# Weights of a fused attention and Mish feed-forward kernel, loaded in quarters along the first slots

## The chip, the cores and the metric

The kernel runs on one core of one Trainium2 chip. The metric is the device time of one launch in microseconds. A core has TensorE (matmuls; in the profile PE, and PEld for its weight loads), VectorE (DVE), ScalarE (ACT), GpSimd (POOL) and SyncE (SP), each with its own queue of instructions, and 16 DMA engines that all transfers share. Here SP issues the loads of q, k and v and the stores of the output, and GpSimd issues the loads of the weights.

## The reference

```
# q, k, v: [8, 12, 448, 64] f32;  w_in: [768, 2048], w_out: [2048, 768] f32
scores = (q @ k.T) / 8
m = max(scores);  e = exp(scores - m)
attn = e / (sum(e) + exp(-m) + 1e-9)          # "softmax off by one"
o = attn @ v                                  # [8, 12, 448, 64]
x = o with heads side by side                 # [3584, 768]
h = x @ w_in                                  # [3584, 2048]
g = h * tanh(softplus(h))                     # Mish
out = g @ w_out                               # [3584, 768] f32
```

## The kernel before

A *pair* is two heads of one batch entry; there are 8 × 6 = 48 pairs, and one *slot* of the schedule for each, with one more at the end. The order of every engine's instructions is the program's own order (`manual_schedule`); each engine works its queue from the front, and waits where a tile that it needs is not ready or a buffer that it writes is not free.

For one pair `load(j)` issues seven transfers on SP: main part and tail of q, k and v (the tail of v in two), into staging tiles of the pool `stage`, three buffers of each. `do_cast(j)` turns them into bf16 on GpSimd (L102 to L112; the bf16 values of v go into one of four tiles `v_aug`, which must be free of the attend of four pairs earlier). `transposes(j)` (L125, L129) brings q and k on TensorE into PSUM, VectorE copies them out (L134, L137). `scores(j, 0)` and `scores(j, 1)` (L149, L161) give the scores in PSUM tiles of which there are two, and ScalarE takes exp of them (L156, L162). `attend(j)` (L172, L181) multiplies with v, whose tile holds ones beside the values, so that the sum comes along; ScalarE takes ln and exp(−ln) of it (L189, L190) and `normalize(j)` (L200) on VectorE writes pair j's 128 of the 768 rows of x, transposed, for its batch entry.

The expert layers come in *units*: `mm1` (L205) is six matmuls of 448 columns for 128 of the 2048 features, one for each pair of the batch entry, with its result copied to `h_sb` by VectorE (L213), or, for the last entry, straight through Mish on ScalarE (L217, L218). `mm2` is half of a sum over the features, eight matmuls of 384 columns (L248); each second one ends with a copy (L256) and each fourth with a store on SP (L260, L264). `mish(b)` (L233, L234) runs for a whole batch entry, with a change of ScalarE's function table before and after.

In slot j, `slot` emits: `load(j + 3)`, `do_cast(j + 2)`, `scores(j, 0)`, one unit, `transposes(j + 1)`, one unit, `attend(j - 1)`, `scores(j, 1)`, some units, `normalize(j - 1)`, and what is left of the units. Batch entry 0 (slots 0 to 5) has no units. In entry 1, slot 6 has none either, slots 7 to 10 have four `mm1` units each, and after slot 10 comes `mish(0)`. From entry 2 on the first slot carries `mm2` units, too. Slot 48 has no units; after it the 16 direct `mm1` units of the last entry and 12 `mm2` units of the one before are taken in turn, so that the `mm1` units run alone until no more of them than `mm2` units are left; then the last entry's `mm2` units.

The weights are loaded on GpSimd, with the cast to bf16 in the transfer, all at the head of the kernel: behind `do_cast(1)` and ahead of slot 0, which begins with `do_cast(2)`. w_in comes in six transfers of 128 whole rows (L287), w_out in four of 512 rows (L293).

Of the kernel before, what the change touches and what calls it, by code (L numbers as in the profile page):

```python
# [15 lines left out]
def kernel(  # L16
# [14 lines left out]
    B, H, S, D = q.shape  # L31
    d_model, d_ff = moe_w_in.shape
    NPAIR = H // 2
    J = B * NPAIR
# [4 lines left out]
    DM_T = d_model // 128  # L39
    FF_T = d_ff // 128  # L40
# [1 line left out]
    SCALE = 1.0 / float(D) ** 0.5  # L42

    singles = ctx.enter_context(tc.tile_pool(name="singles", bufs=1))
    stage = ctx.enter_context(tc.tile_pool(name="stage", bufs=3))
    half = ctx.enter_context(tc.tile_pool(name="half", bufs=3))
    work = ctx.enter_context(tc.tile_pool(name="work", bufs=2))
    s_pool = ctx.enter_context(tc.tile_pool(name="s_ps", bufs=2, space=PSUM))
# [6 lines left out]
    w_in_sb = singles.tile([128, DM_T, d_ff], BF16, name="w_in_sb")  # L55
# [17 lines left out]
    def load(j):  # L73
        b, h0 = j // NPAIR, 2 * (j % NPAIR)
        tiles = {}
        for name, src in (("q", q), ("k", k), ("v", v)):
            main = stage.tile([128, 2, NT, D], FP32, tag=f"{name}m", name=f"{name}m")
            nc.sync.dma_start(  # L78
                out=main,
                in_=src[b, h0 : h0 + 2, 0:MAIN, :].rearrange("h (p t) d -> p h t d", t=NT),  # L80
            )
            if name == "v":
                tail = stage.tile([128, D], FP32, tag="vt", name="vt")
                for h in range(2):
                    nc.sync.dma_start(
                        out=tail[h * 64 : h * 64 + 64, :], in_=src[b, h0 + h, MAIN:S, :]
                    )
            else:
                tail = stage.tile([64, 2, D], FP32, tag=f"{name}t", name=f"{name}t")
                nc.sync.dma_start(  # L90
                    out=tail, in_=src[b, h0 : h0 + 2, MAIN:S, :].rearrange("h p d -> p h d")
                )
            tiles[name] = (main, tail)
        loaded[j] = tiles

    def do_cast(j):
        tiles = loaded.pop(j)
        got = {}
        for name in ("q", "k"):
            main, tail = tiles[name]  # L100
            mb = half.tile([128, NT, 2, D], BF16, tag=f"{name}mb", name=f"{name}mb")
            nc.gpsimd.tensor_copy(out=mb.rearrange("p t h d -> p h t d"), in_=main)  # L102
            tb = half.tile([64, 2, D], BF16, tag=f"{name}tb", name=f"{name}tb")
            nc.gpsimd.tensor_copy(out=tb, in_=tail)
            got[name] = (mb, tb)
        main, tail = tiles["v"]
        va = v_aug[j % NV]
        vr = va[:, 0 : 2 * NT, :].rearrange("p (t h) c -> p t h c", h=2)
        for h in range(2):
            c = h * D  # L110
            nc.gpsimd.tensor_copy(out=vr[:, :, h, c : c + D], in_=main[:, h, :, :])
            nc.gpsimd.tensor_copy(  # L112
                out=va[h * 64 : h * 64 + 64, 2 * NT, c : c + D],
                in_=tail[h * 64 : h * 64 + 64, :],
            )
        cast[j] = got

    def transposes(j):
        got = cast.pop(j)
        ps = x_pool.tile([128, 1024], BF16, tag="x", name="tr_ps")  # L120
        for i, name in enumerate(("q", "k")):
            mb, tb = got[name]
            for t in range(NT):
                c = i * S + t * 128
                nc.tensor.transpose(  # L125
                    ps[:, c : c + 128], mb[:, t].rearrange("p h d -> p (h d)"), ident
                )
            c = i * S + MAIN
            nc.tensor.transpose(  # L129
                ps[:, c : c + TAIL], tb.rearrange("p h d -> p (h d)"), ident[0:64, 0:64]  # L130
            )
        qk = work.tile([128, S + MAIN], BF16, tag="qk", name="qk")
        kt = k_tail[j % 2]
        nc.vector.tensor_copy(out=qk, in_=ps[:, 0 : S + MAIN])  # L134
        for h in range(2):
            r = slice(h * 64, h * 64 + 64)
            nc.vector.tensor_copy(out=kt[r, r], in_=ps[r, S + MAIN : 2 * S])  # L137
        qk_t[j] = qk
# [100 lines left out]
    def mm2(b, t, n, part):  # L239
        key = (b, t)  # L240
        if n == 0 and part == 0:
            open_o[key] = work.tile([128, d_model], FP32, tag="o_sb", name="o_sb", bufs=3)
        if part == 0:
            open_o[key, n] = m_pool.tile([128, 512], FP32, tag="m", name="o_ps")
        op, o_sb = open_o[key, n], open_o[key]
        for ff in range(part * FF_T // 2, (part + 1) * FF_T // 2):
            lhs = gt_t[b // 2][:, ff, :] if t == NT else gm_t[b][:, ff, t * 128 : (t + 1) * 128]
            nc.tensor.matmul(  # L248
                op[:, 0:HALF],
                lhsT=lhs,  # L250
                rhs=w_out_sb[:, ff, n * HALF : (n + 1) * HALF],
                start=(ff == 0),
                stop=(ff == FF_T - 1),
            )
        if part == 1:
            nc.vector.tensor_copy(out=o_sb[:, n * HALF : (n + 1) * HALF], in_=op[:, 0:HALF])  # L256
            if n == 1:
                if t < NT:
                    rows = out[b * S : b * S + MAIN, :].rearrange("(p t) n -> t p n", t=NT)
                    nc.sync.dma_start(out=rows[t], in_=o_sb)  # L260
                else:
                    for i in range(2):
                        r0 = (b - 1 + i) * S + MAIN
                        nc.sync.dma_start(  # L264
                            out=out[r0 : r0 + TAIL, :], in_=o_sb[i * TAIL : (i + 1) * TAIL, :]
                        )
# [4 lines left out]
    def mm2_units(b):  # L271
        return [
            lambda t=t, n=n, part=part: mm2(b, t, n, part)
            for t in range(NT + b % 2)
            for n in range(2)
            for part in range(2)
        ]

    with tc.manual_schedule():
        nc.scalar.preload_act_table_set("natural_log_exp_and_others")  # L280
        for j in range(3):
            load(j)
        do_cast(0)
        transposes(0)
        do_cast(1)
        for dm in range(DM_T):
            nc.gpsimd.dma_start(  # L287
                out=w_in_sb[:, dm, :], in_=moe_w_in[dm * 128 : (dm + 1) * 128, :]
            )
        n = FF_T // 4  # L290
        for i in range(4):
            f = slice(i * n * 128, (i + 1) * n * 128)
            nc.gpsimd.dma_start(  # L293
                out=w_out_sb[:, i * n : (i + 1) * n, :],
                in_=moe_w_out[f, :].rearrange("(f p) c -> p f c", p=128),
            )

        def slot(j, units):
            def take(n):
                for _ in range(min(n, len(units))):  # L300
                    units.pop(0)()

            if j + 3 < J:
                load(j + 3)
            if j + 2 < J:
                do_cast(j + 2)
            rest = max(0, len(units) - 2)
            if j < J:
                scores(j, 0)
            take(1)  # L310
            if j + 1 < J:
                transposes(j + 1)
            take(1)
            if j >= 1:
                attend(j - 1)
            if j < J:
                scores(j, 1)
            take((rest + 1) // 2)
            if j >= 1:
                normalize(j - 1)  # L320
            take(len(units))

        for p in range(B):
            m1 = mm1_units(p - 1) if p >= 1 else []
            m2 = mm2_units(p - 2) if p >= 2 else []
            for i in range(NPAIR):
                if i == 0:
                    units, m2 = m2[:4], m2[4:]
                elif i < 5:
                    units, m1 = m1[:4], m1[4:]  # L330
                else:
                    units, m2 = m2, []
                slot(p * NPAIR + i, units)
                if i == 4 and p >= 1:
                    mish(p - 1)
                    first, m2 = m2[:8], m2[8:]
                    for u in first:
                        u()
        slot(J, [])
        m1 = mm1_units(B - 1, direct=True)  # L340
        m2 = mm2_units(B - 2)
        while m1 or m2:
            if m1:
                m1.pop(0)()
            if m2 and len(m2) >= len(m1):
                m2.pop(0)()
        for u in mm2_units(B - 1):
            u()
# [30 lines left out]
```

## Time and profile before

| | |
|---|---|
| three runs | 547.76 us median (545.96 to 547.79) |
| the profiled execution | 548.19 us, of which the span of the profile 546.4 us |
| TensorE busy | 483.3 us (88%), 2768 matmuls |
| ScalarE, VectorE, GpSimd busy | 297.9, 206.3, 130.2 us |
| chain that ended last | TensorE 82% of the span, ScalarE 6%, DMA 6% |
| moved by DMA | 50.85 MB, of which the weights' queue 6.29 MB |
| granted TensorE clock, mean | 0.961 |

The span is what the profiler saw from the first to the last instruction; the time of the execution is 1.79 us longer. Busy time counts a matmul to its modelled end. In rows in order of time, the first number is the start in us, the second the time from the start to the end of the group, and the bracket at the end of a row says how long the engine was idle before it and what it then got.

### The profile page before, as it was taken

To read this page: it belongs to the slowest core of one execution; us is meant where nothing else is said; L and a number is where in the kernel's file an instruction comes from. 1 tells how busy PE (TensorE), PEld (TensorE's weight loads), DVE (VectorE), ACT (ScalarE), POOL (GpSimd) and SP (SyncE) were. 2 spreads that over 40 slices of the span, in tenths; PEclk is the share of its full clock that TensorE was granted. 3 is DMA by queue.
4 is the path that set the end of the run, shared out by engine and by line. 5 is a ranking of instruction groups with operands and counts; after the bars stand their busy time and mean duration, and the time that the engine had idled before them with its cause. 6 is when DMAs were issued, how large, how long until landed. Compare 5 with 4: busy or idle time off the path is not lost.

```text
span 546.4 us, 7802 instructions
## 1 busy us (share of the span) xinstructions
PE 483.3 (88%) x2768; PEld 234.0 (43%) x2768; DVE 206.3 (38%) x414; ACT 297.9 (55%) x419; POOL 130.2 (24%) x400
## 2 busy tenths in 40 slices
PE   4354779948999799999999899999997999989996
PEld 1111224413445344555445444554453544535553
DVE  3012224622553245524553255434552365220121
ACT  3034464595567555765658556855577465752200
POOL 5413533230230323112420333013311330000000
PEclk9999869986999899999999899999999999989999
DMA  5999554200530434034511353035503420110012
GB/s 135 212 218 219 149 151 120 67 2 0 138 95 30 130 99 134 1 110 126 152 33 54 106 147 86 31 108 149 134 1 112 120 59 1 59 29 31 29 59 86
DMA packets 67783, 50.85 MB, mean 93 GB/s; under 512 B 24480, under 2 KB 63392, under 8 KB 67744
## 3 DMA queue, kind: packets, MB, share of 16 engines
q1 hardware_dynamic: 64768, 44.06, 28.8%
q0 software_dynamic: 2976, 6.29, 6.1%
q8 instruction: 21, 0.34, 0.3%
q14 instruction: 18, 0.15, 0.1%
HBM read 45.61 MB, written 11.01 MB: 104 GB/s over the span
## 4 chain that ended last, share of the span: by engine, by line
PE 82%; ACT 6%; DMA 6%; SPq 3%; DVE 1%; issue 1%; POOL 0%; POOLq 0%
PE o_ps L248 28%; PE h_ps L205 28%; PE av_ps L172 10%; PE s_ps L149 6%; PE tr_ps L125 4%; DMA km<-in_k_dram 3%; PE av_ps L181 3%; DMA kt<-in_k_dram 2%; PE tr_ps L129 2%; PE s_ps L161 2%; ACT e L156 2%; ACT ln L189 1%; ACT rc L190 1%; SPq L78 1%; ACT gm L233 1%
## 5 line engine op out<-in xcount | busy, mean ns | idle before, releaser
L205 PE MATMUL h_ps<-xT,w_in_sb 128*128 128x448 bf16 x768 | 164.7, 358 | 2.0 <-DVE xT L200 2.0
L189 ACT ACTIVATE ln<-av_ps 64x448 f32<-64x448 f32 x96 | 51.7, 539 | 172.9 <-PE av_ps L181 171.7
L156 ACT ACTIVATE e<-s_ps 128x896 bf16<-128x896 f32 x144 | 126.0, 909 | 22.5 <-PE s_ps L149 20.1
L248 PE MATMUL o_ps<-w_out_sb,gm 128*128 128x384 bf16 x768 | 134.9, 333 | 0.0
L213 DVE COPY h_sb<-h_ps 128x448 f32<-128x448 f32 x112 | 70.0, 625 | 97.0 <-PE h_ps L205 96.1
L205 PEld LDWEIGHTS <-w_in_sb 128*128 128x128 bf16 x768 | 71.2, 99 | 68.4 <-issue 12.0
L248 PEld LDWEIGHTS <-gm 128*128 128x128 bf16 x768 | 75.3, 99 | 53.0 <-issue 5.1
L200 DVE TENSOR_TENSOR xT<-av_ps,rc 64x448 bf16<-64x448 f32 x96 | 59.7, 622 | 74.9 <-ACT rc L190 72.6
L149 PE MATMUL s_ps<-qk 64*128 64x448 bf16 x288 | 52.8, 384 | 27.1 <-ACT e L156 26.1
L256 DVE COPY o_sb<-o_ps 128x384 f32<-128x384 f32 x56 | 31.2, 557 | 100.1 <-PE o_ps L248 99.5
L102 POOL CAST qmb<-qm 128x384 bf16<-128x384 f32 x48 | 24.4, 508 | 141.9 <-DMA qm<-in_q_dram 135.3
L134 DVE COPY qk<-tr_ps 128x832 bf16<-128x832 bf16 x48 | 28.4, 591 | 61.1 <-PE tr_ps L129 58.9
L233 ACT ACTIVATE gm<-h_sb 128x1536 bf16<-128x1536 f32 x28 | 39.2, 1470 | 0.1
L149 PEld LDWEIGHTS <-qk 64*128 64x128 bf16 x288 | 14.5, 96 | 52.2 <-issue 51.0
L125 PE MATMUL tr_ps<-ident,qmb 128*128 128x128 bf16 x144 | 17.9, 240 | 14.5 <-POOL qmb L102 14.5
L190 ACT ACTIVATE rc<-ln 128x448 f32<-128x448 f32 x48 | 27.7, 576 | 1.5
L102 POOL CAST kmb<-km 128x384 bf16<-128x384 f32 x48 | 24.3, 505 | 16.4 <-DMA km<-in_k_dram 16.2
L162 ACT ACTIVATE e<-s_ps 128x448 bf16<-128x448 f32 x48 | 25.7, 536 | 0.0
L125 PE MATMUL tr_ps<-ident,kmb 128*128 128x128 bf16 x144 | 18.1, 242 | 6.5 <-POOL kmb L102 6.5
L125 PEld LDWEIGHTS <-qmb 128*128 128x128 bf16 x144 | 12.2, 106 | 25.8 <-POOL qmb L102 16.1
L248 PE MATMUL o_ps<-w_out_sb,gt 128*128 128x384 bf16 x128 | 22.3, 326 | 0.0
L217 ACT ACTIVATE gm<-h_ps 128x384 bf16<-128x384 f32 x16 | 7.9, 491 | 25.7 <-PE h_ps L205 25.7
(58 smaller groups left out, 338.5 us busy)
## 6 DMA issues: line engine op xcount, KB each, us to landing
qm<-in_q_dram SPq DMA_DIRECT2D x48, 192.0 KB, 2.6
km<-in_k_dram SPq DMA_DIRECT2D x48, 192.0 KB, 2.7
vm<-in_v_dram SPq DMA_DIRECT2D x48, 192.0 KB, 2.7
out_dram<-o_sb SPq DMA_DIRECT2D x24, 384.0 KB, 2.7
w_in_sb<-in_moe_w_in_dram POOLq DMA_DIRECT2D x6, 512.0 KB, 11.5
w_out_sb<-in_moe_w_out_dram POOLq DMA_DIRECT2D x4, 768.0 KB, 26.9
qt<-in_q_dram SPq DMA_DIRECT2D x48, 32.0 KB, 2.6
kt<-in_k_dram SPq DMA_DIRECT2D x48, 32.0 KB, 2.8
```

The source lines that it names most:

```text
L102: nc.gpsimd.tensor_copy(out=mb.rearrange("p t h d -> p h t d"), in_=main)
L125: nc.tensor.transpose(ps[:, c : c + 128], mb[:, t].rearrange("p h d -> p (h d)"), ident)
L149: nc.tensor.matmul(sp[:, h, 0:S], lhsT=qk[r, S + t * 128 : S + (t + 1) * 128], rhs=qk[r, 0:S], start=True, stop=True,)
L156: nc.scalar.activation(out=e[:, 2 * t : 2 * t + 2, :], in_=sp[:, :, 0:S], func=AF.Exp, scale=SCALE)
L172: nc.tensor.matmul(av[h][:, 0:S], lhsT=va[:, 2 * t + h, :], rhs=e[:, 2 * t + h, :], start=(t == 0), stop=False,)
L189: nc.scalar.activation(out=ln[r, :], in_=av[h][o, 0:S], func=AF.Ln, bias=1.0)
L190: nc.scalar.activation(out=rc, in_=ln, func=AF.Exp, scale=-1.0)
L200: nc.vector.tensor_mul(x_t[b][r, hp, :], av[h][r, 0:S], rc[r, :])
L205: nc.tensor.matmul(hp[:, 0:S], lhsT=w_in_sb[:, dm, ff * 128 : (ff + 1) * 128], rhs=x_t[b][:, dm, :], start=(dm == 0), stop=(dm == DM_T - 1),)
L213: nc.vector.tensor_copy(out=h_sb[:, ff, :], in_=hp[:, 0:S])
L233: nc.scalar.activation(out=gm[:, f, :], in_=h_sb[:, f, 0:MAIN], func=AF.Mish)
L248: nc.tensor.matmul(op[:, 0:HALF], lhsT=lhs, rhs=w_out_sb[:, ff, n * HALF : (n + 1) * HALF], start=(ff == 0), stop=(ff == FF_T - 1),)
```

## The change

`stage` gets four buffers instead of three, four pairs are loaded ahead of slot 0, and slot j issues `load(j + 4)`. The weight transfers leave the head. Slots 1 to 4 issue a quarter of w_in each behind their `do_cast`: all 768 rows, 512 of the 2048 columns, in one transfer. Slots 6 to 9 issue a quarter of w_out each, with the same 512 rows as before. Slot 6 takes two `mm1` units and, by the flag `late`, emits both at its very end, behind `normalize(5)`; slot 10 then has two instead of four. The last slot takes four `mm2` units of the last entry but one: two ahead of its attend, one behind it, one behind its normalize; 8 are left for the loop that follows.

```diff
-    stage = ctx.enter_context(tc.tile_pool(name="stage", bufs=3))
+    stage = ctx.enter_context(tc.tile_pool(name="stage", bufs=4))
...
-        for j in range(3):
+        for j in range(4):
             load(j)
         do_cast(0)
         transposes(0)
         do_cast(1)
-        for dm in range(DM_T):
+
+        def load_w_in(i):
+            c = slice(i * d_ff // 4, (i + 1) * d_ff // 4)
             nc.gpsimd.dma_start(
-                out=w_in_sb[:, dm, :], in_=moe_w_in[dm * 128 : (dm + 1) * 128, :]
-            )
-        n = FF_T // 4
-        for i in range(4):
-            f = slice(i * n * 128, (i + 1) * n * 128)
+                out=w_in_sb[:, :, c], in_=moe_w_in[:, c].rearrange("(m p) f -> p m f", p=128)
+            )
+
+        def load_w_out(i):
+            n = FF_T // 4
             nc.gpsimd.dma_start(
                 out=w_out_sb[:, i * n : (i + 1) * n, :],
-                in_=moe_w_out[f, :].rearrange("(f p) c -> p f c", p=128),
-            )
+                in_=moe_w_out[i * n * 128 : (i + 1) * n * 128, :].rearrange(
+                    "(f p) c -> p f c", p=128
+                ),
+            )
 
-        def slot(j, units):
-            def take(n):
+        def slot(j, units, late=False):
+            def take(n, last=False):
+                if late and not last:
+                    return
                 for _ in range(min(n, len(units))):
                     units.pop(0)()
 
-            if j + 3 < J:
-                load(j + 3)
+            if j + 4 < J:
+                load(j + 4)
             if j + 2 < J:
                 do_cast(j + 2)
+            if 1 <= j <= 4:
+                load_w_in(j - 1)
+            if 6 <= j <= 9:
+                load_w_out(j - 6)
...
-            take(len(units))
+            take(len(units), last=True)
...
             for i in range(NPAIR):
-                if i == 0:
+                late = p == 1 and i == 0
+                if late:
+                    units, m1 = m1[:2], m1[2:]
+                elif i == 0:
                     units, m2 = m2[:4], m2[4:]
...
-                slot(p * NPAIR + i, units)
+                slot(p * NPAIR + i, units, late)
...
-        slot(J, [])
+        m2 = mm2_units(B - 2)
+        slot(J, m2[:4])
+        m2 = m2[4:]
         m1 = mm1_units(B - 1, direct=True)
-        m2 = mm2_units(B - 2)
```

## Rows read from the trace of the kernel before

**Rows 1.** Page, the span in 40 slices of 13.66 us: TensorE, GpSimd, granted clock
```profile
PE  4354779948999799999999899999997999989996
...
POOL 5413533230230323112420333013311330000000
PEclk9999869986999899999999899999999999989999
```
**Rows 2.** Waits, whole span: us in total, times, longest
```profile
PE tr_ps L125 <- POOL qmb L102: 14.5, 4, 9.3
...
PE tr_ps L125 <- POOL kmb L102: 6.5, 4, 2.7
```
**Rows 3.** In order of time, slots 0 and 1: start, us, engine, line, operation
```profile
7.09 0.62 SPq L90 DMA_DIRECT2D kt<-in_k_dram  x1
...
10.37 0.23 PE L129 MATMUL tr_ps<-ident,ktb 64*128 64x64 bf16 x1
...
11.49 0.62 SPq L90 DMA_DIRECT2D kt<-in_k_dram  x1
11.66 3.34 POOL L287 DMA_DIRECT2D w_in_sb<-in_moe_w_in_dram  x6
...
20.90 0.74 POOL L293 DMA_DIRECT2D w_out_sb<-in_moe_w_out_dram  x1 [2.04 <-DMA w_in_sb<-in_moe_w_in_dram]
...
22.24 0.50 PE L125 MATMUL tr_ps<-ident,qmb 128*128 128x128 bf16 x3 [9.26 <-POOL qmb L102]
...
23.36 0.23 PE L129 MATMUL tr_ps<-ident,ktb 64*128 64x64 bf16 x1
...
26.57 0.56 PE L181 MATMUL av_ps<-e,v_aug_84 64*128 64x448 bf16 x2
```
**Rows 4.** DMA queues, 12 to 53 us: packets, MB, share; one issue row
```profile
q0 software_dynamic: 2976, 6.29, 80.7%
q1 hardware_dynamic: 4719, 2.55, 26.2%
...
km<-in_k_dram SPq DMA_DIRECT2D x4, 192.0 KB, 11.5
```
**Rows 5.** In order of time, slots 2 to 4
```profile
35.39 0.50 PE L125 MATMUL tr_ps<-ident,kmb 128*128 128x128 bf16 x3 [2.75 <-POOL kmb L102]
...
39.59 0.55 PE L181 MATMUL av_ps<-e,v_aug_86 64*128 64x448 bf16 x2
...
51.25 0.56 PE L181 MATMUL av_ps<-e,v_aug_88 64*128 64x448 bf16 x2
...
59.57 0.56 PE L181 MATMUL av_ps<-e,v_aug_90 64*128 64x448 bf16 x2
```
**Rows 6.** In order of time, end of slot 6 to start of slot 9
```profile
78.26 1.27 DVE L200 TENSOR_TENSOR xT<-av_ps,rc 64x448 bf16<-64x448 f32 x2 [4.37 <-ACT rc L190]
...
79.09 0.80 PE L149 MATMUL s_ps<-qk 64*128 64x448 bf16 x4 [1.74 <-ACT e L156]
...
82.46 2.09 PE L205 MATMUL h_ps<-xT,w_in_sb 128*128 128x448 bf16 x6
...
88.67 0.71 PE L149 MATMUL s_ps<-qk 64*128 64x448 bf16 x4
...
96.69 0.71 PE L149 MATMUL s_ps<-qk 64*128 64x448 bf16 x4
```
**Rows 7.** In order of time, end of slot 10
```profile
110.36 2.43 PE L205 MATMUL h_ps<-xT,w_in_sb 128*128 128x448 bf16 x12
...
111.69 0.90 ACT L156 ACTIVATE e<-s_ps 128x896 bf16<-128x896 f32 x1
```
**Rows 8.** In order of time, a second-layer run and the last slot
```profile
463.38 10.56 PE L248 MATMUL o_ps<-w_out_sb,gm 128*128 128x384 bf16 x64
...
482.80 0.36 PE L181 MATMUL av_ps<-e,v_aug_90 64*128 64x448 bf16 x2
...
486.26 5.44 PE L205 MATMUL h_ps<-xT,w_in_sb 128*128 128x448 bf16 x19 [2.05 <-DVE xT L200]
```

## The prediction, made before the result was known

> **What bounds the kernel now.** I read the 40 slices first: TensorE is at 9 or more tenths over most of the span, but only between 2 and 7 tenths in the first six slices, some 80 us [rows 1]. So time is to be had there, and in single later holes; where TensorE is full, the change takes no matmul away. Next, TensorE's waits for casts on GpSimd: 14.5 us for q, the longest 9.3, and 6.5 for k, four times each in the whole span [rows 2], and cut to the first 80 us the view gives the same two rows. The order of time then shows what GpSimd did before the longest one: six w_in and four w_out transfers are issued from 11.66 to 21.64 us, and only then comes the cast that pair 2's transposes want; TensorE idles 9.26 us [rows 3]. The DMA view of 12 to 53 us shows the second half of the same cause: the weights take 80.7% of sixteen engines and the loads 26.2%, together more than full [rows 4], and pairs 3 and 4 come late, so TensorE waits for casts of k, 2.75 us in slot 2 [rows 5]. Last the end: the gap of 2.05 us before the last pass of the first layer goes on [rows 8].
>
> **Terms.** A slot is one pair; I measure it from the end of one attend (the two half matmuls of line 181) to the next. The ends before are 27.13 (slot 1), 40.14 (slot 2), 51.81 (slot 3), 60.13 us (slot 4) [rows 3, 5]: slots 2, 3 and 4 take 13.01, 11.67 and 8.32 us. 8.32 us is the pace without a late load; then the chain attend, ln, reciprocal, exp, scores, transposes sets it, not the transfers.
>
> **1. Weights leave the head of GpSimd's queue.** Pair 2's cast now stands directly behind pair 1's. For pair 1, with free DMA engines, the last k transposes start 10.37 − 7.09 = 3.28 us after the issue of the k tail; pair 2's is issued at 11.49, so its last transpose starts at 14.77, and the attend behind it ends 26.57 + 0.56 − 23.36 = 3.77 us later, at 18.54 instead of 27.13 [rows 3]. **−8.59 us.** SP's issues up to there don't change: the fourth load stands directly behind the third either way.
>
> **2. Slots 2 and 3 go at 8.32 us**, if pairs 3 and 4 land in time: −4.69 and −3.35, **−8.04 us.** Is that so with a quarter of w_in behind each cast? Cost of one w_in quarter in slots 1 to 4, one w_out quarter in slots 6 to 9: all weights took 80.7% of 41 us = 33.1 us of the engines, so an eighth takes 4.1 us if it goes by bytes. Loads: 26.2% of 41 us = 10.7 us for four pairs, so 2.7 us a pair. Sum 6.8 us in a slot of 8.32: it fits, with little over. Upper bound: a column quarter is cut into 768 rows (784 packets with its completions) instead of 128 long rows a transfer; if each cost what a packet of the weights cost on average, 33.1 us × 16 / 2976 = 178 ns [rows 4], a quarter takes 49 × 178 = 8.7 us, and the slot wants 11.4 us of DMA, 3.1 too many. I take the lower one, since the bytes are the same; the upper end could cost 4 × 3.1 us in each of the two groups of four slots. It is softened because SP issues a pair in about 4.4 us (the k tails follow each other by 11.49 − 7.09) against 8.32 us of use, so that a slot's worth of loads stands ready by then: about 4 us a group, +8 in all. Below: if TensorE's rate rises in these slots (first rival).
>
> The issues themselves: a w_out transfer of 512 rows is 0.74 us of GpSimd [rows 3], one of 768 rows by its share of rows some 1.1. One a slot stands behind that slot's cast, and queued behind it is the next pair's cast, a slot early. From the fifth slice on GpSimd is at 5 tenths or less [rows 1], so I take zero on the path; 1.1 us a slot if that cover were gone; below zero nothing, since TensorE doesn't wait for GpSimd there.
>
> **3. Loads 4 ahead, four buffers.** SP runs ahead of the program already, held by buffers and completions, and no transpose waits for a cast after the first 80 us (the two rows again). Taken: 0; bounds −0.5 to +0.5 us, a fraction of one wait of the early ones (14.5 + 6.5 us over eight).
>
> **4. Two first-layer units at the end of slot 6.** All but the last of the first unit's six matmuls fill the hole before scores (1.74 us idle at 79.09); the last needs normalize, which ends at 78.26 + 1.27 = 79.53. Seven matmuls come behind that: 7/6 × 2.09 = 2.44 us at the lower rate, 7/12 × 2.43 = 1.42 us at the higher, and slot 7's scores start at 80.95 to 81.97 instead of 79.09 [rows 6, 7]: +1.86 to +2.88 us. Given back: slot 7 took 88.67 − 79.09 = 9.58 us, slot 8 with the same four units 8.02 [rows 6]; the difference of 1.56 us is the lower rate at slot 7's start (six matmuls in 2.09 us against twelve in 2.43). With work in the hole before it, I expect slot 7 at the higher rate. **+1.32 us** (2.88 − 1.56); bounds +0.3 to +2.9.
>
> The two units are missing in slot 10. They lay beside the chain: twelve matmuls from 110.36 to 112.79 while ScalarE runs from ln to the exp that ends at 111.69 + 0.90 = 112.59, for which slot 11's scores wait anyway [rows 7]. Mish follows on ScalarE behind that exp. **0**; at best −0.2, the difference of the two ends.
>
> **5. Four second-layer units move into the last slot.** Two go before the last attend, one behind it, one behind normalize, and 8 remain for the loop instead of 12: no matmul more or less. Before, TensorE had five matmuls after the attend (end 483.16) and then idled 2.05 us for normalize until 486.26, after which 19 matmuls took 5.44 us against 19/12 × 2.43 = 3.85 at the full rate [rows 7, 8]. Between lie 3.10 us; now two units (64 such matmuls back to back took 10.56 us, so eight take 1.32) and the five of the first layer (1.0 us) offer 3.6 us of work for it. No hole, and so no slow stretch: −2.05 − 1.59 = **−3.64 us.** What is late next there: nothing but TensorE itself. At worst, if the slow stretch stays, −2.05.
>
> **Sum**: −8.59 − 8.04 + 1.32 − 3.64 = −18.95 us, against the profiled execution's 548.19 us (span 546.4 and 1.79 around it): 529.2. That execution lies 0.43 above the median of the runs (547.76), so I predict **528.8 us**; the likeliest case alone 525 to 533, from the bounds of 3 to 5 and about ±1 us for TensorE's changes of rate elsewhere.
>
> **Rivals.**
> *TensorE at the higher rate in the pair-only slots.* The first four slices give the granted clock as 9, yet an attend's two half matmuls take 0.56 us there against 0.36 at the end [rows 3, 5, 8], the pace of the lower level of 1.2 GHz; the next two slices give 8 and 6 [rows 1]. Without the three waits, slots 2 to 6 are denser. At the higher level a slot without units would take slot 8's 8.02 less the two units on its chain, 2 × 1.2 = 5.6 us, 2.7 less than 8.32; five slots −13.6, 515 us; half of them 522. Against it: from 60 to 80 us three such slots ran without a late load, and the granted clock still sat below full there. The Trainium skill, "TensorE: Matmul & The Clock Gate", Part 1: The HAM clock gate, says that the low clock is the default state and that activity releases it. By that rule denser slots should rise to 2.4 GHz and this rival's time would hold; the trace agrees only where units fill the slot (slot 8).
> *Contention stays.* The upper price of a quarter holds: +8 us, 537 us. For it: the DMA engines were more than full with weights under way [rows 4]. Against it: the same bytes are spread over 70 us instead of 41.
> *The other side: slower.* One mechanism: every slot that carries a quarter goes at slot 2's and 3's pace, (13.01 + 11.67) / 2 = 12.34 us, since each load then queues behind weight packets. Eight slots × 4.02 = +32 on the sum: 561 us. It turns slower from 18.95 / 4.02, that is five of the eight slots. For it: the short rows; against: two slots alone had the pace, with all ten weight transfers queued at once.
> *The end doesn't give.* The hole only moves behind the added units: 532.4 us.
>
> **Numbers.** Forecast 0.70; higher rate 0.10; contention 0.10; the end 0.06; slower side 0.03; and 0.01 that the early wait merely moves. Range 519 to 537: it leaves out the whole of the slower side, and parts of the higher rate and of contention. About 0.5% (2.7 us) is what a measurement can tell from no change: faster 0.95, same 0.02, slower 0.03.
>
> **What would show it.** Right: no wait of TensorE for a GpSimd cast above 1 us after 12 us; the attend of slot 1 ends near 18.5, that of slot 4 near 43.5 (18.54 + 3 × 8.32) instead of 60.13; DMA share in 22 to 60 us at 8 tenths (6.8 of 8.32), not full; slot 7's scores near 65 (79.09 − 16.63 + 2.88); no 2 us hole before the last first layer. Wrong: casts of k still late in slots 2 to 5 (contention), slots of 6 us (rate), a slot 6 above 11 us (late units), or second-layer units that push the last attend out without closing the hole.

## The result, and the profile after

The changed kernel takes 526.96 us in the median (523.89 to 527.19) beside 547.6 us (four runs of the kernel before; the 547.76 above is of three): a ratio of 0.9617, 95% interval 0.9577 to 0.9657, so 3.4 to 4.2% faster. The profiled execution has a span of 525.3 us, 21.1 below the one before.

The page, its slices first (13.1 us each here). TensorE's second and third slices, 3 and 5 tenths before [rows 1], are at 7 and 6 now:

```profile
PE   4767899479997999999997999999997999999996
...
POOL 4544542303311133023311133023311220000000
PEclk9856799769999999999999899999999999999999
DMA  5799998004404351055404351055404400110022
```

Its waits, whole span, against [rows 2]. 3.8 of the 4.5 us are the very first load, at the start of the kernel; no other wait for a cast is above 1.0 us:

```profile
PE tr_ps L125 <- POOL qmb L102: 4.5, 2, 3.8
...
PE tr_ps L125 <- POOL kmb L102: 1.9, 3, 1.0
```

The three waits for a cast of k all lie ahead of the first weight transfer; this is the last of them:

```profile
14.26 0.50 PE L125 MATMUL tr_ps<-ident,kmb 128*128 128x128 bf16 x3 [0.44 <-POOL kmb L102]
```

In order of time, slots 1 to 3, to be read beside [rows 3, 5]: pair 2's cast now starts at 12.24 and not at 21.68 (before, the second fence); its k transposes end at 14.9; the attends end at 18.46, 26.20 and 34.54 (before 27.13, 40.14, 51.81). The first weight transfer is issued at 20.40:

```profile
12.24 0.51 POOL L102 CAST qmb<-qm 128x384 bf16<-128x384 f32 x1 [0.50 <-DMA qm<-in_q_dram]
...
14.70 0.23 PE L129 MATMUL tr_ps<-ident,ktb 64*128 64x64 bf16 x1
...
17.91 0.55 PE L181 MATMUL av_ps<-e,v_aug_84 64*128 64x448 bf16 x2
...
20.40 0.96 POOL L289 DMA_DIRECT2D w_in_sb<-in_moe_w_in_dram  x1
...
25.65 0.55 PE L181 MATMUL av_ps<-e,v_aug_86 64*128 64x448 bf16 x2
...
33.98 0.56 PE L181 MATMUL av_ps<-e,v_aug_88 64*128 64x448 bf16 x2
```

```profile
21.68 0.50 POOL L102 CAST qmb<-qm 128x384 bf16<-128x384 f32 x1
```

End of slot 6 to slot 8, beside [rows 6]. The two late units are the x5 and x7 groups: five matmuls, a hole of 1.03 us until normalize ends, seven matmuls in 1.48 us; slot 7's scores start at 63.59 and slot 8's at 71.45:

```profile
58.52 0.56 PE L181 MATMUL av_ps<-e,v_aug_86 64*128 64x448 bf16 x2
...
59.72 1.42 PE L205 MATMUL h_ps<-xT,w_in_sb 128*128 128x448 bf16 x5
62.17 1.48 PE L205 MATMUL h_ps<-xT,w_in_sb 128*128 128x448 bf16 x7 [1.03 <-DVE xT L200]
63.59 0.55 PE L149 MATMUL s_ps<-qk 64*128 64x448 bf16 x4
...
71.45 0.71 PE L149 MATMUL s_ps<-qk 64*128 64x448 bf16 x4
```

The last slot, beside [rows 8]: two units (x16) stand behind the attend, and the first layer follows them with no wait, at full rate (48 matmuls in 9.26 us):

```profile
468.19 0.36 PE L181 MATMUL av_ps<-e,v_aug_90 64*128 64x448 bf16 x2
468.49 2.77 PE L248 MATMUL o_ps<-w_out_sb,gm 128*128 128x384 bf16 x16
...
471.10 9.26 PE L205 MATMUL h_ps<-xT,w_in_sb 128*128 128x448 bf16 x48
```

Three marks, from the chain and the order of time, say where the 21.1 us came from. "First Mish" is the table load of the first Mish, behind slot 10; "steady" the start of the first run of 64 second-layer matmuls to that of the sixth; "end" from there to the start of the last 128. Their rows in the chain, before and then after:

```profile
113.04 1.28 ACT L233
...
169.41 10.40 PE o_ps L248 x64
...
463.54 10.40 PE o_ps L248 x64
...
520.92 20.81 PE o_ps L248 x128
```

```profile
95.81 1.28 ACT L233
...
152.33 10.40 PE o_ps L248 x64
...
446.42 10.40 PE o_ps L248 x64
...
499.83 20.82 PE o_ps L248 x128
```

| | before | after | difference |
|---|---|---|---|
| first Mish | 113.04 | 95.81 | −17.23 |
| first run of 64 | 169.41 | 152.33 | −17.08 |
| steady | 294.13 | 294.09 | −0.04 |
| end | 57.38 | 53.41 | −3.97 |

### The profile page after: what moved, and what is told of

It reads as the page before. It is cut to its first block, busy times and chain, and to the rows that moved or that the text cites. A ratio compares the mean times of both kernels' runs of the same rounds, so it can differ in the third digit from the quotient of the medians.

```text
span 525.3 us, 7796 instructions
## 1 busy us (share of the span) xinstructions
PE 480.2 (91%) x2768; PEld 233.1 (44%) x2768; DVE 206.3 (39%) x414; ACT 297.7 (57%) x419; POOL 128.4 (24%) x398
## 4 chain that ended last, share of the span: by engine, by line
PE 87%; ACT 7%; DVE 2%; SPq 2%; issue 1%; DMA 1%; POOL 0%
PE o_ps L248 29%; PE h_ps L205 29%; PE av_ps L172 11%; PE s_ps L149 6%; PE tr_ps L125 4%; PE av_ps L181 3%; PE tr_ps L129 2%; PE s_ps L161 2%; ACT e L156 2%; ACT ln L189 2%; ACT rc L190 1%; ACT gm L233 1%; DVE qk L134 1%; SPq L78 1%; SPq L90 1%
## 5 line engine op out<-in xcount | busy, mean ns | idle before, releaser
L205 PE MATMUL h_ps<-xT,w_in_sb 128*128 128x448 bf16 x768 | 161.5, 354 | 1.0 <-DVE xT L200 1.0
L111 POOL CAST v_aug_84<-vm 128x192 bf16<-128x192 f32 x24 | 8.2, 344 | 76.3 <-PE av_ps L172 72.6
L111 POOL CAST v_aug_88<-vm 128x192 bf16<-128x192 f32 x24 | 8.2, 344 | 75.6 <-PE av_ps L172 73.3
L111 POOL CAST v_aug_90<-vm 128x192 bf16<-128x192 f32 x24 | 8.3, 344 | 62.0 <-PE av_ps L172 61.4
```

Source lines behind the costliest of these rows:

```text
L205: nc.tensor.matmul(hp[:, 0:S], lhsT=w_in_sb[:, dm, ff * 128 : (ff + 1) * 128], rhs=x_t[b][:, dm, :], start=(dm == 0), stop=(dm == DM_T - 1),)
```

## The experiments

The times of a group of runs stand beside their own runs of the kernel before. Of a single profile the same three marks are used, since the steady part differs by some 1.6 us from one execution to the next with TensorE's rate (294.1 us in the profiles above, 292.5 in the one of after's second run below). The edits are shown shortened; words in them stand for code that is left out. The intervals behind the ratios are 95% intervals.

**The weights alone.** The kernel before with `load_w_in` and `load_w_out` in slots 1 to 4 and 6 to 9 as in the change, and nothing else of it.

```
-    (ten weight transfers ahead of slot 0)
+    if 1 <= j <= 4: load_w_in(j - 1)      # in slot j, behind do_cast(j + 2)
+    if 6 <= j <= 9: load_w_out(j - 6)
```

> The kernel before with the weight transfers alone moved (quarters in slots 1 to 4 and 6 to 9); three staging buffers, loads 3 ahead, no units in slot 6, none in the last slot. Theory: the head's gain is all from the weights' place. In the trace of after, TensorE reaches the table load of the first Mish 17.2 us earlier (95.81 against 113.04), and the late units cost and give back about the same, so 547.6 - 17.2 = 530.4 us, between 529.5 and 531.5. Rival, the fourth buffer and the earlier loads carry a part: pairs 4 to 7 come late in slots 2 to 5, at least two slots stay at some 12 us instead of 8.3: 534 to 538 us.

531.0 us beside 546.16 (0.9711, 0.9672 to 0.9751). First Mish at 96.43, −16.6; slots 1 to 3 end at 18.55, 26.30, 34.62, as in after. The 0.6 us that are missing lie in slot 7 (10.30 us from attend to attend, in after 9.68), behind the last wait for a cast. So the head's gain is all from the weights' place; the fourth buffer and the earlier loads add nothing.

**The earlier loads alone.**

```
-    stage = ... bufs=3      for j in range(3): load(j)      load(j + 3)
+    stage = ... bufs=4      for j in range(4): load(j)      load(j + 4)
```

> The kernel before with four staging buffers and loads 4 ahead alone; weights at the head as before. Theory: 547.6 us, within 0.5: pair 2's cast still stands behind the ten weight transfers, and pairs 3 and 4 still share the DMA engines with them, since SP issues no load earlier than before there. Rival, the lead was what slots 2 and 3 lacked: they go at 8.3 us, 539.6 us.

547.62 us beside 546.16 (1.0021, 0.9997 to 1.0045); first Mish at 113.63, and the wait of 9.5 us for pair 2's cast is still there. No gain, as forecast.

**All weights in one burst, behind pair 2's cast.** The kernel after with no weight transfer in slots 1 to 9 and

```
+    if j == 0:
+        for i in range(4): load_w_in(i)
+        for i in range(4): load_w_out(i)
```

> The kernel after, but all eight weight transfers in one burst in slot 0, behind the cast of pair 2. Theory (two causes of about 8.6 us each, the queue and the shared DMA engines): slot 1 keeps its gain (attend ends at 18.5 us), but the weights again fill the DMA engines for some 40 us from 17 us on, and about three of slots 2 to 5 go at some 12.3 us instead of 8.3: 527 + 3 x 4 = 539 us, 534 to 543. Rival (only the queue counted): 527 to 529 us, as after. Rival (only the DMA engines counted): 547 us, with slot 1 long.

533.34 us beside 547.41 (0.9759, 0.9722 to 0.9797), some 7 above after. Slot 1 keeps its gain (18.62); slots 2 to 6 take 9.4, 8.1, 8.3, 10.5 and 11.6 us, and first Mish comes at 103.28, 7.5 later than in after. Both causes are real and the rivals with one cause fall. The price of the shared engines was two slots (5 and 6), not about three, and the time lies just below the range forecast, 534 to 543. Slot 2's 9.4 us is the queue once more: the eight issues hold GpSimd until 22.51, and TensorE waits 0.91 us for pair 3's cast of q. The casts of k in order of time, pairs 4 to 7, show how: with the engines full, k comes every 9 to 12 us and is used every 8.3, so it takes until pair 6 before TensorE feels it:

```profile
30.02 0.51 POOL L102 CAST kmb<-km 128x384 bf16<-128x384 f32 x1 [1.71 <-DMA km<-in_k_dram]
38.86 0.51 POOL L102 CAST kmb<-km 128x384 bf16<-128x384 f32 x1 [1.76 <-DMA km<-in_k_dram]
49.55 0.51 POOL L102 CAST kmb<-km 128x384 bf16<-128x384 f32 x1 [2.29 <-DMA km<-in_k_dram]
61.30 0.51 POOL L102 CAST kmb<-km 128x384 bf16<-128x384 f32 x1 [2.42 <-DMA km<-in_k_dram]
```

TensorE's waits for pair 3's q and for the k of pairs 6 and 7:

```profile
23.12 0.50 PE L125 MATMUL tr_ps<-ident,qmb 128*128 128x128 bf16 x3 [0.91 <-POOL qmb L102]
...
50.12 0.50 PE L125 MATMUL tr_ps<-ident,kmb 128*128 128x128 bf16 x3 [1.87 <-POOL kmb L102]
...
61.86 0.50 PE L125 MATMUL tr_ps<-ident,kmb 128*128 128x128 bf16 x3 [2.69 <-POOL kmb L102]
```

**The same burst with three buffers, loads 3 ahead.**

> The run with all weights in one burst behind pair 2's cast, with three staging buffers and loads 3 ahead. There slots 5 and 6 were 2.2 and 3.3 us long and slots 3 and 4 not. Theory: loads that ran ahead covered the first two slots, and the fourth buffer gives one slot of this cover, so with three buffers one slot more is long: 536 to 538 us. Rival (SP gets no further ahead there, held by completions and not by buffers): 533 us, within 1.5.

534.45 us beside 545.94 (0.9798, 0.9774 to 0.9823), slots 2 to 6 of 9.7, 8.3, 8.0, 10.8 and 11.3 us, first Mish at 103.30. The fourth buffer gives no cover even here; the theory of one slot of cover a buffer fell. The two traces bear the rival out: SP's issues wait for loads of k to land for 7.5 us with four buffers and 7.6 with three in the first 62 us, and the issues from 25 us on stand at the same times to 0.5 us (a load of k at 36.83 in both).

**w_in by whole rows.** The kernel after with the six old transfers of 128 rows, spread over slots 1 to 4.

```
-    one transfer of all rows, columns c, in each of slots 1 to 4
+    for dm in ((0, 1), (2,), (3, 4), (5,))[i]: (the old transfer of rows dm)
```

> The kernel after with w_in in its six transfers of 128 whole rows, two, one, two and one in slots 1 to 4. Theory: the spread in time is what counts, not the cut by columns, since slot 6's units come long after the last transfer: 527 us as after, 525.5 to 528.5. Rival (the packet size has its price): the long rows take the engines less time, slots 4 and 5 change, and the time moves by 2 us or more.

525.43 us beside 547.41 (0.9605, 0.9576 to 0.9634), first Mish at 96.10: by its ratio the same as after (0.9617). The cut by columns is worth nothing on the clock. It has a price off the path: the weights' queue takes 7.7% of the engines' span with column quarters, 6.9% with rows (of 525 us: 40 and 36 us).

**Without the two late units.**

```
-    late = p == 1 and i == 0;  if late: units, m1 = m1[:2], m1[2:]
+    late = False               # slot 6 none, slots 7 to 10 four units each
```

> The kernel after without the two late units: slot 6 has none, slots 7 to 10 four each. Theory: they cost slot 6 1.9 us (slot 7's scores come 4.51 us after the attend instead of 2.60) and give slot 7 1.7 us back (7.86 us instead of 9.58), so without them slot 6 is short and slot 7 long again: 526.9 us, 526 to 528, and slot 7 takes about 9.5 us. Rival A, they are pure cost, slot 7 is at the higher rate anyway: 525.1 us and slot 7 at 7.9 us. Rival B, they shorten slot 10 and bring Mish forward: 529 us.

525.61 us beside 546.16 (0.9621, 0.9584 to 0.9658), by its ratio the same as after, though the time itself lies under the forecast 526 to 528 and near rival A's 525.1; slot 7 speaks for the theory. Its scores come 2.59 us after the attend and it takes 9.60 us, in sum 12.19, against 4.51 + 7.86 = 12.37 in after:

```profile
58.32 0.56 PE L181 MATMUL av_ps<-e,v_aug 64*128 64x448 bf16 x2
...
61.47 0.99 PE L149 MATMUL s_ps<-qk 64*128 64x448 bf16 x4 [1.74 <-ACT e L156]
...
71.07 0.71 PE L149 MATMUL s_ps<-qk 64*128 64x448 bf16 x4
```

So in these two profiles this part of the change is a trade at par, as the theory had it. It needn't be so in each execution: in the profile with two units ahead of the last attend (below), which has no late units either, slot 7 goes at the higher rate on its own, 8.00 us from attend to attend against 9.49 before.

**The end alone**, with four units, with two ahead of the attend, with two behind it (the kernel before otherwise):

```
-    slot(J, [])
+    slot(J, m2[:4])         # and 8 left;  or m2[:2] ahead;  or m2[:2] behind normalize
```

> The kernel before with the end alone changed: four second-layer units in the last slot, 8 in the loop. Theory: the hole of 2.05 us and the slow stretch behind it go, whatever lies ahead: 547.6 - 4.0 = 543.6 us (in after the start of the last 128 matmuls moved by 21.09 us, that of the run of 64 before it by 17.12). Rival, the end gains only because the pattern of TensorE's rate was shifted by the head: 545.5 to 547.6 us, with a slow stretch still behind the last attend.

> The kernel before with only two second-layer units in the last slot, both ahead of its attend; 10 stay for the loop. Theory (the end gains because work stands between the last attend and normalize): nothing stands there now but five matmuls, so the hole of 2.05 us and the slow stretch stay, a little later: no change against before, within 0.5 us. Rival (moving units out of the loop is itself the gain): half of the gain of the run with four units, 1.8 us less than before.

> The kernel before with two second-layer units in the last slot, both behind its normalize in every queue, so between the last attend and the first layer on TensorE; none ahead. Theory (the work between attend and normalize is what counts): the hole of 2.05 us closes and no slow stretch follows, 3.6 us less than before, as with four units. Rival, from the run with two units ahead, which kept the hole but had no slow stretch in its profile: the slow stretch depends on what runs ahead of the attend, and with none there it stays: 2.0 us less than before.

Ratios 0.9927 (0.9900 to 0.9953), 0.9956 (0.9931 to 0.9982) and 0.9955 (0.9934 to 0.9975). The "end" stretch of the three profiles is 53.41, 55.62 and 53.49 us, against 57.38. The first layer's matmuls behind the last attend, in order of time, one fence for each of the three kernels in that order (four, two ahead, two behind):

```profile
487.82 7.36 PE L205 MATMUL h_ps<-xT,w_in_sb 128*128 128x448 bf16 x38
```

```profile
484.57 6.03 PE L205 MATMUL h_ps<-xT,w_in_sb 128*128 128x448 bf16 x31 [2.05 <-DVE xT L200]
```

```profile
485.26 6.98 PE L205 MATMUL h_ps<-xT,w_in_sb 128*128 128x448 bf16 x36
```

With four units, and with two behind, the hole is gone and the matmuls go at 0.19 us each; with two ahead the hole of 2.05 us is where it was, to the hundredth. That is the theory's half. Its other half fell: it said that the slow stretch (19 matmuls in 5.44 us, [rows 8]) comes with the hole and that two units ahead change nothing, but in this profile 31 matmuls behind the same hole take 6.03 us, full rate, the stretch is 1.76 us shorter with the hole in it, and the time is 1.0 to 3.8 us less than before (the rival had 1.8).

Why the rate held there is open. The "end" is 57.38 us in all three profiles with the old end (before, the weights alone, the loads alone), so it may be what runs ahead of the attend. But the execution itself differed: its steady part takes 292.51 us, that of the other three 294.05 to 294.15, so TensorE's rate fell at other places in it. No run separates the two. With that it is open, too, whether the end is worth 2 us or nearly 4 in the median (the three intervals span 1.0 to 5.5 us); two units behind normalize, forecast at 3.6 us less and by the rival at 2.0, gave 1.4 to 3.6.

**The transposes in another PSUM pool.** The kernel after with

```
-    ps = x_pool.tile([128, 1024], BF16, tag="x", name="tr_ps")
+    ps = (m_pool, tag "m") if j <= 7 else (x_pool, tag "x")
```

> The kernel after, with the transposes of pairs 0 to 7 in a PSUM tile of the expert layers' pool, idle there, instead of the pool that attend uses. Theory: with the loads in time the chain of a slot without units contains the wait of attend's second matmul for VectorE's copies out of the transposes' tile (it starts 1.07 us after the first, 0.66 us more than a matmul apart, in slots 1 to 6): six slots shorter by 0.66, 527 - 4 = 523 us, 522 to 524.5. Rival (something else of the slot ends just as late): 526 us or more.

520.11 us beside 547.41 (0.9512, 0.9483 to 0.9540), 6 to 7 below after. In after, the first of attend's six matmuls and the rest (slot 3):

```profile
30.93 0.56 PE L172 MATMUL av_ps<-e,v_aug_88 128*128 128x448 bf16 x1
...
32.00 2.05 PE L172 MATMUL av_ps<-e,v_aug_88 128*128 128x448 bf16 x5 [0.51 <-DVE k_tail_92 L137]
```

and with the other pool (lines are 3 higher there; slot 4):

```profile
36.01 2.42 PE L175 MATMUL av_ps<-e,v_aug 128*128 128x448 bf16 x6
```

The wait is gone, and slots 2 to 6 take 6.9 to 7.2 us instead of 7.7 to 8.3. The gain is more than the forecast 4 us: with the hole closed TensorE also runs at the higher of its two rates in part of each slot (granted clock 0.74 to 0.82 of full in slots 2 to 6, in after 0.50 in three of them; transposes of 0.34 us where they took 0.50), and first Mish comes at 90.00, 5.8 earlier.

**A version that beats both.** Besides the other pool (now in every slot with no unit ahead of attend), the twelve second-layer units of entries 2, 4 and 6 lie as 2, 8, 2:

```
+    elif p >= 2 and p % 2 == 0 and i == 0:
+        late = True;  units, m2 = m2[:2], m2[2:]      # was 4, on and off the chain
...
+    late = p >= 2 and p % 2 == 0                      # last slot of the entry: 2, was 0
```

> The kernel after once more, beside the next three: 527.0 us, 525.5 to 528.5.

> A version meant to beat both: the kernel after with the transposes of slots that have no unit behind them in the expert layers' PSUM pool (slots 0 to 6, 11, and those below), and in batch entries 2, 4 and 6 with the twelve second-layer units as 2, 8 and 2 instead of 4, 8 and 0: two at the end of the first slot, two at the end of the last, where TensorE waits for ScalarE's chain. Theory: the pool gives 7 us as alone; a unit behind attend lies beside ScalarE's ln, reciprocal and exp (2.5 us, two units) while one ahead of it is on the chain, so each of three entries gets 2.4 us shorter: 527 - 7 - 7 = 513 us, 510 to 516. Rival (TensorE is full in these entries, moving units gives nothing): 519 to 521 us.

After again: 526.65 us (0.9646, 0.9623 to 0.9669). The new version: **509.07 us** beside 545.94 (0.9324, 0.9303 to 0.9346). In after, entry 2's last slot has TensorE waiting for ScalarE's exp, and the eight matmuls behind it take 2.74 us, the lower rate:

```profile
169.04 0.94 PE L149 MATMUL s_ps<-qk 64*128 64x448 bf16 x4 [2.11 <-ACT e L156]
169.91 2.74 PE L248 MATMUL o_ps<-w_out_sb,gm 128*128 128x384 bf16 x8
```

In the new one two units (x16) fill that place, and the next eight take 1.47:

```profile
156.59 2.76 PE L251 MATMUL o_ps<-w_out_sb,gm 128*128 128x384 bf16 x16
159.28 0.55 PE L152 MATMUL s_ps<-qk 64*128 64x448 bf16 x4
159.77 1.47 PE L251 MATMUL o_ps<-w_out_sb,gm 128*128 128x384 bf16 x8
```

The steady part goes from one run of 64 to the next in 56.75 or 56.76 us, five times; in after that was 57.45 to 59.34. That makes 283.8 us of 294.1: the rival with a full TensorE falls, and the time lies just under the forecast 510 to 516. How the 10.3 us divide is not shown: the other pool, too, takes a wait out of these slots (the attend in entry 2's last slot waits 0.71 us for VectorE's copies in after), and units and pool were not run apart there.

## Why the prediction was right

The predicted 528.8 us lies 1.8 above the measured 526.96; the range held it. By its steps, from the two profiles:

| step | predicted | measured | from |
|---|---|---|---|
| 1, slot 1 | −8.59 | −8.67 | attend ends 18.46, was 27.13 |
| 2, slots 2 and 3 | −8.04 | −8.60 | 7.74 + 8.34 us, were 13.01 + 11.67 |
| slots 4 to 6 | 0 | −0.14 | attends 34.54 to 59.08 and 51.81 to 76.49 |
| 4, late units | +2.88 | +1.91 | scores 4.51 us after the attend, were 2.60 |
| 4, slot 7 | −1.56 | −1.72 | 7.86 us, was 9.58 |
| 4, slot 10 | 0 | −0.09 | 7.93 us, was 8.02 |
| 5, the end | −3.64 | −3.97 | the table above |

The sum is −21.3. Of it 0.15 us is given back between first Mish and the first run of 64, and 0.08 is the difference between the steps up to first Mish, read on TensorE (−17.31), and the mark itself, read on ScalarE (−17.23): the span's 21.1.

*Step 1 and 2, the mechanism:* shown by the runs. The weights alone give 16.6 of 17.2 us, the loads alone nothing, and the burst brings the second cause back while most of the first stays away.

*Step 2, the price of a quarter:* mis-sized, without harm. The DMA view of after, 20 to 45 us:

```profile
q0 software_dynamic: 2352, 2.36, 61.4%
q1 hardware_dynamic: 5160, 2.84, 43.4%
```

2.36 MB are three quarters of w_in, 61.4% of 25 us is 15.4 us of the engines, so 5.1 us a quarter: above the 4.1 by bytes, below the 8.7 by packets. A pair costs 2.6 us there (43.4% of 25 us for 2.84 MB, at 0.69 MB a pair); by bytes the 2.7 of the prediction were 2.9, since its window held 3.7 pairs and not four. The engines were full, not at 8 tenths as I wrote: over the 22 to 60 us that I had named, their share is 1.04. So that sign failed, and with it my reason that the transfers leave the engines a little room. What kept the path free is the lead of the loads, by which I had softened only the upper bound: with the weights under way no transpose waits for a cast of k at all, with four buffers or with three (the weights alone).

*Step 4:* seven matmuls behind normalize took 1.48 us and not 2.44; I had taken the lower rate for them, and TensorE was at the higher one by then. That term is 1.0 of the 2.1 us by which the sum was short; 0.6 is slot 2, part of it at the higher rate, and 0.3 the end.

*Step 5:* right in size in this profile, half right in its reason: the work behind the attend closes the hole, but the slow stretch does not follow from the hole, as the runs on the end show.

*The rivals:* the higher rate in the slots without units came in pieces only (slots 2 and 5 took 7.74 and 7.89 us at a granted clock of 0.78 and 0.72, the others 8.3 at 0.50). The sentence on the clock that stood with it (the Trainium skill, "TensorE: Matmul & The Clock Gate", Part 1: The HAM clock gate: low by default, released by activity) agrees with the trace once the slots are denser still: with the other PSUM pool they take 6.9 to 7.2 us at a granted clock of 0.74 to 0.82. Contention was there, but stayed below the path, and the slower side got nowhere near.

## What to carry to other kernels

A bulk load that shares an engine's queue with small work of the critical chain costs twice, once in the queue and once in the DMA engines; move it behind the work that is wanted first, and spread it so that load and bulk together stay under the slot's time (here 2.6 and 5.1 us of 8.3). A gap in the busiest engine is worth filling with work that is wanted later anyway, but only where the chain waits for something else: beside ScalarE's ln and exp two units cost nothing, ahead of attend they are on the chain. When the transfers no longer bind, look at which buffer the next matmul waits for.

## What the runs showed that I had not expected

- The slow stretch after a 2.05 us hole is no property of the hole alone: 19 matmuls in 5.44 us in one profile, 31 in 6.03 in another behind a hole of the same length. Whether the work ahead or the execution made the difference is open.
- Four buffers and three were alike in every pair of runs, even with full DMA engines (533.34 and 534.45 us, first Mish at 103.28 and 103.30).
- Loads beside column quarters came faster than beside w_out's rows of 768 columns: k every 8.8 us at first in the burst (30.02 to 38.86), every 11.8 later in it (49.55 to 61.30) and every 11.6 before (34.82 to 46.38). The weights' packets are 1.0 KB on average in the first of these stretches and 1.5 KB in the other two. That shorter packets of the weights let the loads in more often would explain it; it was not tried.
- A wait of 0.51 us a slot for a PSUM buffer was worth over 1 us a slot in slots 3, 4 and 6, where TensorE's rate rose with it.
